# Transposing attention weights by products with a diagonal in the opening of a fused attention and two-MLP kernel

## The chip, the cores and the metric

One core of a Trainium2 chip runs the kernel. The metric is the device time of one execution in microseconds (us). Times of several executions are given as their median. A profiled execution has its own time, and beside it the span from its first to its last instruction.

The engines go by short names: PE is TensorE (PEld its weight loads), DVE VectorE, ACT ScalarE, POOL GpSimd, SP SyncE, which here issues nearly all DMAs. Each engine works through its own queue in order.

## The reference

Sliding-window attention with four sink positions, then two MLPs, all float32:

```python
scores = (1 / sqrt(D)) * q @ k.T                 # B, H, S, D = 2, 8, 768, 64
keep = (key < 4) | ((0 <= query - key) & (query - key < 128))
scores = where(keep, scores, -1e9)
a = exp(scores - max(scores))
a = a / (sum(a) + 1e-9)
x = (a @ v)                                      # heads joined: 1536 x 512
h = x @ w_in;  x = (max(h, 0) + alpha * min(h, 0)) @ w_out    # first MLP, d_ff = 2048
h = x @ w_in2; out = (h - tanh(h)) @ w_out2                   # second MLP
```

The weights reach the device as float64 bits, two 32-bit words each, and are turned into float32 there.

## The kernel before

The 1536 tokens are twelve blocks of 128 (NU); a block has eight heads, taken two at a time. Such a pair is a step n, 48 in all (NPAIR). The MLP work goes in chunks of 512 tokens (c) and tiles of 128 hidden units (f). Float32 precision in the big products comes from splitting each operand into a high and a low part.

A step of attention passes through these functions:

- `s_mm(n)` (L274; L268 for the first block): scores of pair n on PE into two PSUM tiles `ps_o`. Keys and queries come in groups G of two pairs, split by `kq_hi` (ACT, L238) and `kq_lo` (DVE, L241).
- `s_max(n, a)` (DVE, L283): mask and running maximum of one head, result in `pq`; then `s_exp(n, a)` (ACT, L292): exponential and row sum.
- `norm_sum(n)`: 1e-9 is added to the two sums on POOL (L298), reciprocal on DVE (L300). `norm(n)` (DVE, L307) multiplies both heads' rows by the reciprocal. `sink_copy(n)` (DVE, L313) gathers the sink columns of two pairs.
- `t_mm(n)` (PE, L324): the normalised rows are transposed, four 128x128 transposes against an identity matrix (two in a sequence's first block), into `ps_t` or `ps_h`; `sink_mm` (L346) transposes the sink columns. `t_ev(n)` (ACT, L331) copies the transposed tile to `pt`, `sink_ev` (ACT, L350) the sinks to `pts`.
- `pv(n)` (PE, L363, L364): value products; in every second pair of the later blocks also the sink products (L367). `x_h` (ACT, L374) and `x_l` (DVE, L379) split the finished block into the first MLP's input.

The opening is a loop over n from 0 to 18 (S_LEAD = 19) with attention alone. The program order is written out by hand, and each engine's queue follows it. In step n PE gets `s_mm(n+1)`, then `keep_busy` (L513, products of zeros whose result nobody reads, eight, one, three and then two of them), `t_mm(n-1)` and `pv(n-2)`. Three tiles of the first MLP's weights are converted in between (CONV0, from steps 6, 10 and 14): two passes on ACT (L73, L75) and two on DVE (L77, L79). From the end of the loop on, a second loop mixes MLP products (L396, L448) with the remaining attention steps; its first MLP product is the 128x512 product of L396 that waits for `x_h` of block 3.

The lines that set the order on PE in the opening:

```python
            if not last:
                s_mm(n + 1)
                tps[n - 1] = ps_tile("th" if n < S_LEAD - 3 else "ht"[n % 2])
                keep_busy({0: 8, 1: 1, 2: 3}.get(n, 2), tps[n - 1])
...
                if not last:
                    t_mm(n - 1)
...
            if 2 <= n < S_LEAD - 2:
                pv(n - 2)
```

Of the kernel before, what the change touches and what calls it, by code (L numbers as in the profile page):

```python
# [9 lines left out]
F32 = mybir.dt.float32  # L10
# [11 lines left out]

S_LEAD = 19
CONV0 = ((0, 6), (1, 10), (2, 14))
B, H, S, D = 2, 8, 768, 64
# [8 lines left out]
SINK = 32  # L34
# [32 lines left out]

def convert_scaled(nc, pair, dst, seen):

    lw, hw = pair[:, :, 0], pair[:, :, 1]  # L70
    top = pair.bitcast(U16)[:, :, 1]
    di = dst.bitcast(I32)
    nc.scalar.activation(out=dst, in_=hw.bitcast(F32), func=AF.Abs, scale=W_UP, accum_out=seen)  # L73
    yield
    nc.scalar.activation(out=lw, in_=top, func=AF.Copy, scale=1.0 / 8192, bias=FLOOR)  # L75
    yield
    nc.vector.scalar_tensor_tensor(di, di, 3, lw, op0=ALU.logical_shift_left, op1=ALU.bitwise_or)  # L77
    yield
    nc.vector.scalar_tensor_tensor(di, hw, SIGN, di, op0=ALU.bitwise_and, op1=ALU.bitwise_or)  # L79
# [58 lines left out]
def fast_path(tc, qk, v, vsink, limits, w1i, w1o, alpha, w2i, w2o, out, outer):  # L138
# [3 lines left out]
    with ExitStack() as ctx:  # L142
# [60 lines left out]
        def conv_w(m, f):  # L203
            raw = stage[m][f % 2]
            if m == 1 and f < 3:
                wf[m, f] = ap.tile([128, 1024], F32, name="wf", tag="wx" if f == 2 else "pq", bufs=1 if f == 2 else 2)
            else:
                wf[m, f] = wp.tile([128, 1024], F32, name="wf", tag="wf", bufs=NF)
            at = m * NF + f
            yield from convert_scaled(nc, raw.rearrange("p (n t) -> p n t", t=2), wf[m, f], seen[:, at:at + 1])  # L210

# [15 lines left out]
        x_t, y_t = {}, {}  # L227
        pq, sums, ptb, pts, vps, sks, sps, tps = {}, {}, {}, {}, {}, {}, {}, {}
        initial = [True]
# [84 lines left out]

        def t_mm(n):
# [35 lines left out]

        def pv(n):
            u, p, b, i, w = geom(n)
# [5 lines left out]
            for a in range(2):  # L359
# [4 lines left out]
                nc.tensor.matmul(d, lhsT=vt[u][:, h * D:(h + 1) * D], rhs=pt[:, a, 1, :], start=p == 0 and i == 0, stop=p == 3 and i < 2)  # L364
            if p % 2 == 1 and i >= 2:
                for pp in (p - 1, p):
                    nc.tensor.matmul(o[:, pp, :], lhsT=vs[:, pp, :], rhs=pts[G], start=False, stop=pp == 3)  # L367

# [210 lines left out]

        def norms(n):  # L580
            norm_sum(n, 0)
            norm_sum(n, 1)
            norm(n)
            sink_copy(n)

        s_mm(0)
        for n in range(S_LEAD):
            last = n == S_LEAD - 1
            a_loads(n)
            if n == 0:  # L590
                kq_hi(0)
            if n in (3, 5):
                s_max(n, 0)
                s_max(n, 1)
                kq_lo(n // 2 + 1)
                if n == 3:
                    k_sinks(0)
# [4 lines left out]
            if n >= 2:  # L602
                t_ev(n - 2)
                if 5 <= n < S_LEAD - 2:
                    splits_hi(n)
            if n not in (3, 5):
                s_max(n, 0)
                s_max(n, 1)
            if n == 1:
                kq_lo(0)  # L610
            if n == 4:
                kq_lo(1)
                k_sinks(1)
            if n >= 6 and not last:
                splits_lo(n - 1)
# [4 lines left out]
            if n in (1, 2):  # L620
                kq_hi(n)
            if n == 4:
                kq_hi(3)
            if n == S_LEAD - 2:
                pv(n - 2)
            if n >= 1:
                norms(n - 1)
                if not last:
                    t_mm(n - 1)
                    if has_sinks(n - 1):  # L630
                        sink_mm(n - 1, n + 1)
            if 2 <= n < S_LEAD - 2:
                pv(n - 2)
            for f, at in CONV0:
                if n == at:
                    conv_start(0, f, 1)
                if n == at + 1:
                    conv_step(0, f)
            if n >= 5 and n % 4 == 1:
                x_h(n - 2)  # L640
            if last:
# [7 lines left out]
            for f, at in CONV0:  # L649
                if at + 1 < n < at + 4:  # L650
                    conv_step(0, f)
# [434 lines left out]
```

## Time and profile before

| | us |
|---|---|
| median of 3 runs | 648.95 (648.41 to 650.08) |
| the profiled execution | 648.51 |
| its span | 646.7 |
| PE busy | 632.7 (98% of the span) |
| DVE busy | 520.6 (81%) |
| ACT busy | 469.6 (73%) |
| POOL busy | 24.2 (4%) |

A span lies some 2 us below the time of its execution. Busy time of PE counts each matmul up to a modelled end, so that overlapping tails can make it look full; the starts of its instructions say more than its busy share. In a timeline a row is a run of like instructions of one engine: start, length from the first start to the last end, engine, line, operation, tiles, and in brackets the idle time before it with what ended that.

### The profile page before, as it was taken

The page shows a single profiled execution, that of the slowest core. Times are in us where ns is not written, and L with a number is a line of the kernel's source. Part 1 is how long each engine was busy: PE and PEld are TensorE (multiplying, and loading weights), DVE is VectorE, ACT ScalarE, POOL GpSimd, SP SyncE. Part 2 cuts the span into 40 slices and gives each one's busy share as a digit, 9 for nine tenths or more (in the row PEclk, how much of TensorE's full clock was granted, in tenths as well). Part 3 has the DMA queues.
Part 4 walks back from the last instruction along what each step waited for, and adds up shares of the span by engine and source line. Part 5 has one row for each costly group of instructions (what it writes and reads, how often), then busy time and mean ns, then how long its engine had stood idle before and what let it go on. Part 6 is the DMA issues. An engine that isn't in the chain of part 4 may idle for free.

```text
span 646.7 us, 9269 instructions
## 1 busy us (share of the span) xinstructions
PE 632.7 (98%) x3245; PEld 499.5 (77%) x3245; DVE 520.6 (81%) x1046; ACT 469.6 (73%) x936; POOL 24.2 (4%) x57
## 2 busy tenths in 40 slices
PE   8899999999999999999999999999999999999996
PEld 3556777777777777777888888888888888888884
DVE  7998989997676665578999969888898888888883
ACT  6998888886675555568877768777777777777772
POOL 1001101110000000000000000000000000000000
PEclk9999999999999999999999999999999999999998
DMA  5753444651100000323555300000010000100001
GB/s 151 237 184 116 147 166 172 216 162 35 49 3 16 17 1 1 131 71 125 205 195 192 125 1 1 1 1 1 1 66 1 2 2 0 66 0 2 0 2 70
DMA packets 27176, 47.36 MB, mean 73 GB/s; under 512 B 3184, under 2 KB 15728, under 8 KB 27120
## 3 DMA queue, kind: packets, MB, share of 16 engines
q1 hardware_dynamic: 26400, 46.29, 21.1%
q8 instruction: 27, 0.44, 0.3%
q10 hardware_dynamic: 720, 0.39, 0.2%
q14 instruction: 29, 0.24, 0.1%
HBM read 43.53 MB, written 3.15 MB: 72 GB/s over the span
## 4 chain that ended last, share of the span: by engine, by line
PE 89%; ACT 3%; DVE 3%; SPq 2%; issue 1%; DMA 1%; POOL 0%; ACTq 0%; DVEq 0%
PE ps_o L448 39%; PE ps_h L396 23%; PE ps_s L396 9%; PE ps_t L396 8%; PE ps_s L274 2%; PE ps_t L324 2%; PE ps_v L363 2%; SPq L177 1%; PE ps_v L364 1%; PE ps_v L367 1%; ACT pq L292 1%; DVE pq L283 1%; DMA raw<-in_moe_w_out_dram 1%; DVE wf L77 1%; DVE pq L307 0%
## 5 line engine op out<-in xcount | busy, mean ns | idle before, releaser
L224 DVE SCALAR_TENSOR_TENSOR wl<-wf,wh 128x512 fp32r<-128x512 f32 x192 | 123.5, 683 | 42.8 <-ACT wh L219 42.8
L219 ACT ACTIVATE wh<-wf 128x512 fp32r<-128x512 f32 x192 | 110.8, 628 | 0.1
L396 PE MATMUL ps_h<-x,wh 128*128 128x512 f32 x296 | 96.4, 406 | 0.4 <-ACT x L374 0.3
L448 PE MATMUL ps_o<-gh,wh 128*128 128x512 f32 x192 | 76.5, 398 | 0.0
L448 PE MATMUL ps_o<-gh,wl 128*128 128x512 f32 x192 | 75.0, 391 | 0.0
L448 PE MATMUL ps_o<-gl,wh 128*128 128x512 f32 x192 | 74.8, 390 | 0.0
L448 PE MATMUL ps_o<-wh,gh 128*128 128x512 f32 x192 | 74.7, 389 | 0.0
L448 PE MATMUL ps_o<-wl,gh 128*128 128x512 f32 x192 | 74.7, 389 | 0.0
L448 PE MATMUL ps_o<-wh,gl 128*128 128x512 f32 x192 | 74.7, 389 | 0.0
L396 PEld LDWEIGHTS ps_h<-x,wh 128*128 128x128 f32 x296 | 52.1, 188 | 11.4 <-issue 1.9
L292 ACT ACTIVATE pq<-pq,nm 128x288 f32<-128x288 f32 (+1 forms) x96 | 48.5, 509 | 14.5 <-DVE nm L283 14.4
L396 PE MATMUL ps_h<-x,wl 128*128 128x512 f32 x148 | 58.4, 394 | 0.4 <-DVE wl L224 0.4
L331 ACT ACTIVATE pt<-ps_t 128x512 f32<-128x512 f32 (+1 forms) x39 | 22.0, 563 | 42.6 <-PE ps_t L324 42.6
L427 ACT ACTIVATE gh<-g 128x512 fp32r<-128x512 f32 x48 | 30.4, 633 | 29.6 <-DVE g L126 29.6
L77 DVE SCALAR_TENSOR_TENSOR wf<-wf,raw 128x1024 int32<-128x1024 int32 x32 | 39.1, 1222 | 7.1 <-ACT raw L75 7.1
L448 PEld LDWEIGHTS ps_o<-gh,wh 128*128 128x128 f32 x192 | 36.1, 188 | 8.4 <-issue 1.4
L448 PEld LDWEIGHTS ps_o<-gh,wl 128*128 128x128 f32 x192 | 36.0, 188 | 7.8
L448 PEld LDWEIGHTS ps_o<-wh,gh 128*128 128x128 f32 x192 | 36.0, 188 | 7.5
L448 PEld LDWEIGHTS ps_o<-wh,gl 128*128 128x128 f32 x192 | 36.0, 188 | 7.5
L448 PEld LDWEIGHTS ps_o<-wl,gh 128*128 128x128 f32 x192 | 36.0, 188 | 7.5
L448 PEld LDWEIGHTS ps_o<-gl,wh 128*128 128x128 f32 x192 | 36.1, 188 | 7.1
L126 DVE COPY_PREDICATED g<-mask,t 128x512 f32<-128x512 int32 x48 | 36.4, 759 | 4.9
(156 smaller groups left out, 1354.0 us busy)
## 6 DMA issues: line engine op xcount, KB each, us to landing
raw<-in_moe_w_in_dram SPq DMA_DIRECT2D x32, 512.0 KB, 3.3
raw<-in_moe_w_out_dram SPq DMA_DIRECT2D x32, 512.0 KB, 4.2
raw_qk<-in_qk_dram SPq DMA_DIRECT2D x92, 64.0 KB, 3.1
vt<-in_v_dram SPq DMA_DIRECT2D x12, 256.0 KB, 3.1
out_dram<-ob SPq DMA_DIRECT2D x2, 1024.0 KB, 4.2
out_dram<-ob SPq DMA_DIRECT2D x3, 256.0 KB, 2.1
vs<-in_vsink_dram SPq DMA_DIRECT2D x2, 256.0 KB, 4.3
raw_qk<-in_qk_dram ACTq DMA_DIRECT2D x4, 64.0 KB, 2.7
```

The lines of the kernel that those rows point to most:

```text
L77: nc.vector.scalar_tensor_tensor(di, di, 3, lw, op0=ALU.logical_shift_left, op1=ALU.bitwise_or)
L126: nc.vector.copy_predicated(g, mask.bitcast(I32), t)
L219: nc.scalar.activation(out=hi, in_=src, func=AF.Copy, scale=W_DOWN)
L224: nc.vector.scalar_tensor_tensor(lo, wf[m, f][:, 512 * part:512 * part + 512], W_DOWN, hi, op0=ALU.mult, op1=ALU.subtract)
L274: nc.tensor.matmul(sps[n, a][:, :w], lhsT=kq[l][h, p, at:at + 128], rhs=kq[r][h, p, K_EVEN:K_EVEN + w], start=e == 0, stop=e == 2)
L292: nc.scalar.activation(out=e, in_=e, func=AF.Exp, scale=-1.0, bias=nm[:, 2 * n + a:2 * n + a + 1], accum_out=sums[G][:, hh:hh + 1])
L324: nc.tensor.transpose(t[:, 256 * a + 128 * e:256 * a + 128 * e + 128], pq[G][:, hh + a, c:c + 128], ident)
L331: nc.scalar.activation(out=ptb[n][:, :, e0:, :], in_=tv[:, :, e0:, :], func=AF.Copy)
L363: nc.tensor.matmul(d, lhsT=vt[u - 1][:, h * D:(h + 1) * D], rhs=pt[:, a, 0, :], start=p == 0, stop=False)
L396: nc.tensor.matmul(h_ps[f], lhsT=w, rhs=x[:, r, kk, :], start=at == 0, stop=at == 11)
L427: nc.scalar.activation(out=gh, in_=mid[f], func=AF.Copy)
L448: nc.tensor.matmul(o, lhsT=l, rhs=r, start=f == 0 and e == 0, stop=f == NF - 1 and e == 2)
```

## The change

- For the pairs n < DIAG = 18 the rows of `pq` are no longer normalised. `norm` makes two diagonal matrices on POOL instead, the identity times the reciprocal of the row sums, and `t_mm` multiplies `pq` with them as float32 products: transposition and scaling in one. `sink_copy` multiplies the sink columns by the reciprocal on DVE.
- For the first three weight tiles the conversion's second pass moves from ACT to DVE, as one pass of tensor_scalar followed by the two-input pass.
- `keep_busy` gets eight, two, four, two and then none.
- The order in the opening is written anew: from step 5 `pv(n-2)` stands ahead of `s_mm(n+1)`, the sink products are a part of their own (`pv_sinks`) behind it, the sums and diagonals of pair n-1 stand between the two maxima of step n, `x_h` stands ahead of the transposes, and the key splits are called from two small tables.

```diff
+DIAG = 18
...
-def convert_scaled(nc, pair, dst, seen):
+def convert_scaled(nc, pair, dst, seen, by_vector=False):
...
+    if by_vector:
+        nc.vector.tensor_scalar(di, di, 4, 1, op0=ALU.logical_shift_left, op1=ALU.logical_shift_right)
+        yield
+        nc.vector.scalar_tensor_tensor(di, lw, 29, di, op0=ALU.logical_shift_right, op1=ALU.bitwise_or)
...
         def norm(n):
             u, p, b, i, w = geom(n)
             G, hh = 2 * u + p // 2, 2 * (p % 2)
+            if n < DIAG:
+                dg[n] = gp.tile([128, 2, 128], F32, name="dg", tag="gg", bufs=6)
+                for a in range(2):
+                    nc.gpsimd.tensor_scalar(dg[n][:, a, :], ident, sums[G][:, hh + a:hh + a + 1], None, op0=ALU.mult)
+                return
...
-                nc.vector.tensor_copy(sks[G], pq[G][:, :, 128:160])
+                if n < DIAG:
+                    nc.vector.tensor_tensor(sks[G], pq[G][:, :, 128:160], sums[G].unsqueeze(2).to_broadcast([128, 4, SINK]), op=ALU.mult)
...
-                    if i > 0 or e == 1:
-                        nc.tensor.transpose(t[:, 256 * a + 128 * e:256 * a + 128 * e + 128], pq[G][:, hh + a, c:c + 128], ident)
+                    d = t[:, 256 * a + 128 * e:256 * a + 128 * e + 128]
+                    if n < DIAG and (i > 0 or e == 1):
+                        nc.tensor.matmul(d, lhsT=pq[G][:, hh + a, c:c + 128], rhs=dg[n][:, a, :], start=True, stop=True)
...
+            if 2 <= n:
+                t_ev(n - 2)
+                if 5 <= n < S_LEAD - 2:
+                    keys_hi(n)
...
+            if n >= 5 and n < S_LEAD - 2:
+                pv(n - 2, False)
...
-                keep_busy({0: 8, 1: 1, 2: 3}.get(n, 2), tps[n - 1])
+                keep_busy({0: 8, 1: 2, 2: 4, 3: 2}.get(n, 0), tps[n - 1])
...
                 s_max(n, 0)
+                if n > 3:
+                    norm_parts(n - 1)
                 s_max(n, 1)
...
+            elif n >= 5 and not last:
+                pv_sinks(n - 2)
+            if n >= 5 and n % 4 == 1:
+                x_h(n - 2)
...
-            if 2 <= n < S_LEAD - 2:
+            if 2 <= n < 5:
                 pv(n - 2)
```

On PE, before, from the scores of step 10 on: scores, idle products, the transposes of pair 9 with its sinks (`sk`), the value products of pair 8 (`pt`, `vt`), the scores of step 11.

```order
L274 MATMUL ps_o<-kq 128x288 x6
L513 LDWEIGHTS idle
L513 MATMUL ps_t<-idle 128x512
L513 LDWEIGHTS idle
L513 MATMUL ps_t<-idle 128x512
L324 MATMUL ps_t<-ident,pq 128x128 x4
L346 MATMUL ps_o<-ident,sk 128x128
L363 MATMUL ps_v<-pt,vt 64x128
L364 MATMUL ps_v<-pt,vt 64x128
L363 MATMUL ps_v<-pt,vt 64x128
L364 MATMUL ps_v<-pt,vt 64x128
L274 MATMUL ps_o<-kq 128x288 x6
```

The value products there are those of the pair before the one just transposed. The same place on PE in the changed kernel, from the scores of step 10 on (`dg` is the diagonal):

```order
L280 MATMUL ps_o<-kq 128x288 x6
L339 MATMUL ps_t<-dg,pq 128x128 x4
L363 MATMUL ps_o<-ident,sk 128x128
L380 MATMUL ps_v<-pt,vt 64x128
L381 MATMUL ps_v<-pt,vt 64x128
L380 MATMUL ps_v<-pt,vt 64x128
L381 MATMUL ps_v<-pt,vt 64x128
L280 MATMUL ps_o<-kq 128x288 x6
L389 MATMUL ps_v<-pts,vs 128x128 x2
L339 MATMUL ps_h<-dg,pq 128x128 x4
```

Now the value products behind the transposes are those of pair 9 itself, the sink products of pair 9 (L389) follow the next scores, and the idle products are gone.

On DVE, before, in step 8: key split, reciprocal and normalisation of pair 7, first DVE pass of a conversion, the two maxima of step 9.

```order
L241 TENSOR_TENSOR kq<-raw_qk,kq 128x2x256
L300 RECIPROCAL sums<-sums 128x2
L307 TENSOR_SCALAR pq<-pq,sums 128x288 x2
L77 SCALAR_TENSOR_TENSOR wf<-wf,raw_90 128x1024
L283 ISA pq,nm<-ps_o,m_even 128x288
L283 ISA nm 128x1
L283 ISA pq,nm<-ps_o,m_even 128x288
```

The same place on DVE in the changed kernel:

```order
L247 TENSOR_TENSOR kq<-raw_qk,kq 128x2x256
L79 SCALAR_TENSOR_TENSOR wf<-raw_90,wf 128x1024
L289 ISA pq,nm<-ps_o,m_even 128x288
L289 ISA nm 128x1
L306 RECIPROCAL sums<-sums 128x2
L289 ISA pq,nm<-ps_o,m_even 128x288
```

The normalisation is gone, the reciprocal stands between the two maxima of the next step, and the conversion's pass here (L79) is the second of three on DVE.

## Rows read from the trace of the kernel before

**Rows 1.** Page, span in 40 slices, busy tenths; PEclk: granted clock, tenths.

```profile
PE   8899999999999999999999999999999999999996
...
DVE  7998989997676665578999969888898888888883
...
PEclk9999999999999999999999999999999999999998
```

**Rows 2.** Windows, four steps: stretch, its length, then busy us (instructions), as headed.

```profile
core 0: us, PE busy (x) PEld busy (x) DVE busy (x) ACT busy (x) POOL busy (x), PEclk, DMA share, GB/s
25.82:36.67 10.85, 9.84 (x86) 6.18 (x86) 10.54 (x36) 10.40 (x30) 1.20 (x5) 1.00 0.71 218
```

**Rows 3.** Timeline of PE, one step: start, length, line, operation, tiles, shapes, count.

```profile
35.74 0.60 PE L324 MATMUL ps_t<-ident,pq 128*128 128x128 f32 x4
...
36.38 0.45 PE L363 MATMUL ps_v<-pt,vt 128*64 128x128 f32 x4
...
36.98 0.67 PE L274 MATMUL ps_o<-kq 64*128 64x288 f32 x6
37.58 0.60 PE L513 MATMUL ps_h<-idle 128*128 128x512 bf16 x2
38.05 0.72 PE L324 MATMUL ps_h<-ident,pq 128*128 128x128 f32 x4
```

**Rows 4.** Timeline of PE, other places; the x3 row is cut by a narrow window.

```profile
16.40 0.53 PE L274 MATMUL ps_o<-kq 64*128 64x288 f32 x4 [1.02 <-DVE kq L241]
...
18.20 0.66 PE L274 MATMUL ps_o<-kq 64*128 64x288 f32 x6
...
45.53 0.71 PE L367 MATMUL ps_v<-pts,vs 128*128 128x128 f32 x4 [0.53 <-ACT pts L350]
...
45.75 0.50 PE L367 MATMUL ps_v<-pts,vs 128*128 128x128 f32 x3
...
46.18 0.66 PE L274 MATMUL ps_o<-kq 64*128 64x288 f32 x6
47.54 0.59 PE L513 MATMUL ps_h<-idle 128*128 128x512 bf16 x2 [0.70 <-ACT pt L331]
...
52.32 0.50 PE L396 MATMUL ps_h<-x,wh 128*128 128x512 f32 x1 [0.25 <-ACT x L374]
```

**Rows 5.** Single lines, 17 to 47 us: duration ns min/median/max, first and last start.

```profile
L324 PE MATMUL ps_h<-ident,pq x24: 272/273/334, 17.3 to 44.1; 128*128 128x128 f32 x24
...
L367 PE MATMUL ps_v<-pts,vs x12: 275/275/377, 34.1 to 46.0; 128*128 128x128 f32 x12
...
L331 ACT ACTIVATE pt<-ps_h x6: 577/591/612, 18.8 to 46.9; 128x512 f32<-128x512 f32 x6
```

**Rows 6.** Groups by line and shape, 0 to 52 us: busy us, mean ns | idle before.

```profile
L292 ACT ACTIVATE pq<-pq,nm 128x288 f32<-128x288 f32 x28 | 14.8, 535 | 0.3 <-DVE nm L283 0.3
...
L307 DVE TENSOR_SCALAR pq<-pq,sums 128x288 f32<-128x288 f32 x26 | 8.5, 367 | 0.5
...
L73 ACT ACTIVATE wf<-raw 128x1024 f32<-128x1024 f32 x3 | 3.4, 1145 | 0.0
```

**Rows 7.** Timeline of ACT: key copy of step 5; evacuation ahead of TensorE's 47.54.

```profile
15.48 0.63 ACT L238 ACTIVATE kq<-raw_qk 128x512 fp32r<-128x512 f32 x1 [0.32 <-DMA raw_qk<-in_qk_dram]
...
46.90 0.59 ACT L331 ACTIVATE pt<-ps_h 128x512 f32<-128x512 f32 x1
```

**Rows 8.** Timelines of POOL, and of DVE around POOL's addition at 38.86.

```profile
2.00 0.29 POOL masks.py:199 TENSOR_SCALAR_AFFINE_SELECT ident<-ident 128x128 f32<-128x128 f32 x1
...
38.86 0.62 POOL L298 TENSOR_SCALAR sums<-sums 128x2 f32<-128x2 f32 x1 [1.99 <-ACT pq L292]
...
46.08 0.21 POOL L298 TENSOR_SCALAR sums<-sums 128x2 f32<-128x2 f32 x1 [3.63 <-ACT pq L292]
...
38.19 1.22 DVE L79 SCALAR_TENSOR_TENSOR wf<-raw,wf 128x1024 int32<-128x1024 int32 x1
```

**Rows 9.** Windows, columns as in rows 2: early in the opening, and after the end.

```profile
10.00:20.00 10.00, 8.07 (x65) 4.84 (x66) 9.31 (x40) 7.06 (x23) 1.19 (x4) 1.00 0.74 235
...
642.00:644.00 2.00, 0.00 (x0) 0.00 (x0) 0.00 (x0) 0.00 (x0) 0.00 (x0) 0.83 0.44 143
```

More of the change, by code (lines that the diff above doesn't have):

```diff
@@ L74, in convert_scaled @@
     yield
-    nc.scalar.activation(out=lw, in_=top, func=AF.Copy, scale=1.0 / 8192, bias=FLOOR)
-    yield
-    nc.vector.scalar_tensor_tensor(di, di, 3, lw, op0=ALU.logical_shift_left, op1=ALU.bitwise_or)
+    if by_vector:
+        nc.vector.tensor_scalar(di, di, 4, 1, op0=ALU.logical_shift_left, op1=ALU.logical_shift_right)
+        yield
+        nc.vector.scalar_tensor_tensor(di, lw, 29, di, op0=ALU.logical_shift_right, op1=ALU.bitwise_or)
+    else:
+        nc.scalar.activation(out=lw, in_=top, func=AF.Copy, scale=1.0 / 8192, bias=FLOOR)
+        yield
+        nc.vector.scalar_tensor_tensor(di, di, 3, lw, op0=ALU.logical_shift_left, op1=ALU.bitwise_or)
     yield
@@ L209, in conv_w @@
             at = m * NF + f
-            yield from convert_scaled(nc, raw.rearrange("p (n t) -> p n t", t=2), wf[m, f], seen[:, at:at + 1])
+            yield from convert_scaled(nc, raw.rearrange("p (n t) -> p n t", t=2), wf[m, f], seen[:, at:at + 1], m == 0 and f < len(CONV0))
         whl = {}
@@ L227, in fast_path @@
         x_t, y_t = {}, {}
-        pq, sums, ptb, pts, vps, sks, sps, tps = {}, {}, {}, {}, {}, {}, {}, {}
+        pq, sums, ptb, pts, vps, sks, sps, tps, dg = {}, {}, {}, {}, {}, {}, {}, {}, {}
         initial = [True]
@@ L322, in t_mm @@
                 for e, c in ((0, 160 - cur), (1, cur)):
-                    if i > 0 or e == 1:
-                        nc.tensor.transpose(t[:, 256 * a + 128 * e:256 * a + 128 * e + 128], pq[G][:, hh + a, c:c + 128], ident)
+                    d = t[:, 256 * a + 128 * e:256 * a + 128 * e + 128]
+                    if n < DIAG and (i > 0 or e == 1):
+                        nc.tensor.matmul(d, lhsT=pq[G][:, hh + a, c:c + 128], rhs=dg[n][:, a, :], start=True, stop=True)
+                    elif i > 0 or e == 1:
+                        nc.tensor.transpose(d, pq[G][:, hh + a, c:c + 128], ident)
         def t_ev(n):
@@ L350, in sink_ev, with pv @@
             nc.scalar.activation(out=pts[n // 2], in_=tps.pop((n, 0))[:, 384:512], func=AF.Copy)
-        def pv(n):
+        def pv(n, sinks=True):
             u, p, b, i, w = geom(n)
@@ L364, in pv, with pv_sinks @@
                 nc.tensor.matmul(d, lhsT=vt[u][:, h * D:(h + 1) * D], rhs=pt[:, a, 1, :], start=p == 0 and i == 0, stop=p == 3 and i < 2)
-            if p % 2 == 1 and i >= 2:
+            if sinks:
+                pv_sinks(n)
+        def pv_sinks(n):
+            u, p, b, i, w = geom(n)
+            if has_sinks(n):
                 for pp in (p - 1, p):
-                    nc.tensor.matmul(o[:, pp, :], lhsT=vs[:, pp, :], rhs=pts[G], start=False, stop=pp == 3)
+                    nc.tensor.matmul(vps[u][:, pp, :], lhsT=vs[:, pp, :], rhs=pts[n // 2], start=False, stop=pp == 3)
         def x_h(n):
@@ L583, in norms, with keys_lo, keys_hi @@
             norm(n)
+        def norms(n):
+            norm_parts(n)
             sink_copy(n)
+        def keys_lo(n):
+            for G in {1: (0,), 2: (1,), 3: (2,), 5: (3,)}.get(n, (n // 2 + 1,) if n > 5 and n % 2 == 0 else ()):
+                kq_lo(G)
+                if G < 2:
+                    k_sinks(G)
+        def keys_hi(n):
+            for G in {0: (0,), 1: (1,), 2: (2,), 4: (3,)}.get(n, (n // 2 + 2,) if n > 4 and n % 2 else ()):
+                kq_hi(G)
         s_mm(0)
@@ L600, in fast_path @@
                 tps[n - 1] = ps_tile("th" if n < S_LEAD - 3 else "ht"[n % 2])
-                keep_busy({0: 8, 1: 1, 2: 3}.get(n, 2), tps[n - 1])
[L602 to L605, printed above, removed]
+                keep_busy({0: 8, 1: 2, 2: 4, 3: 2}.get(n, 0), tps[n - 1])
             if n not in (3, 5):
                 s_max(n, 0)
+                if n > 3:
+                    norm_parts(n - 1)
                 s_max(n, 1)
[L609 to L615, printed above, removed]
+                if n == 1:
+                    keys_lo(n)
             s_exp(n, 0)
@@ L619, in fast_path @@
             s_exp(n, 1)
[L620 to L623, printed above, removed]
+            if n in (1, 4):
+                keys_hi(n)
             if n == S_LEAD - 2:
                 pv(n - 2)
+            elif n >= 5 and not last:
+                pv_sinks(n - 2)
+            if n >= 5 and n % 4 == 1:
+                x_h(n - 2)
             if n >= 1:
-                norms(n - 1)
+                if n <= 3:
+                    norm_parts(n - 1)
+                sink_copy(n - 1)
+                if n == 2 or 6 <= n and not last:
+                    keys_lo(n)
                 if not last:
```

18 lines of the change are left out of this document (8 added, 10 removed).

## The prediction

> **What bounds the kernel now.** I read the page's slices first, then the windows by stretch, then the timelines of TensorE (PE), VectorE (DVE) and ScalarE (ACT) up to the first product of the first MLP. In the slices the reader sees PE at nine tenths almost throughout, and DVE up there with it in the second and third slice of 16 us, in the opening [rows 1]. After the opening PE has next to no holes, so a shift of its first MLP product, which starts at 52.32 us [rows 4], goes to the end of the kernel almost whole. The question is when that product starts.
>
> Inside the opening the pace is one pair of heads ("a step", n) at a time. Two scores products mark it: s_mm(7) starts at 18.20 and s_mm(17) at 46.18, ten steps in 27.98 us, 2.8 us each [rows 4]. The windows show who sets it: in the four steps from 25.82 to 36.67 DVE is busy 10.54 of 10.85 us, ACT 10.40, PE 9.84 (matmul tails counted) [rows 2]. DVE is full, ACT nearly. PE has filler inside: two idle products a step, 0.47 us from their start to the next transpose [rows 3].
>
> The order on PE in that stretch matters most. Transposes of pair n-1 (L324, L346) are followed by the value products of pair n-2 (L363, L364), then by the scores of n+2 (L274) and idle products (L513) [rows 3]. So ACT has a whole step to evacuate the transposes of pair n-1 before PE asks for them.
>
> **The change, part by part.**
>
> *DVE.* Two normalising multiplications a pair go away: 0.367 us each [rows 6], 0.57 us for the two on DVE's queue, so 2.3 us in four steps. The sink copy becomes a two-input multiplication: under 0.1 us more. A conversion gets one more DVE pass (tensor_scalar, 128x1024). No such row exists; it lies between the 128x288 multiplication (0.367) and the two-input pass of 1.22 us on 1024 elements [rows 6, 8]. Either way DVE falls from 10.5 to between 8.7 and 9.6 us in four steps, 2.2 to 2.4 a step. DVE stops being the bound.
>
> *ACT.* Each conversion loses its second pass, which I price like its first, 1.145 us [rows 6], in four steps; ACT falls from 10.40 to about 9.3, or 2.3 a step.
>
> *PE.* A transpose is one matmul record, a float32 product of the same shape two: the code of L367 issues two products a call and the trace has four records [rows 4, 5]. Spacing is the same 0.11 us: (0.60-0.273)/3 for four transposes [rows 3, 5], (0.50-0.275)/2 inside the L367 group [rows 4, 5]. So four transposes (4 x 0.11 = 0.44 to what follows) become eight records (0.87): +0.43 a step. Two idle products less from step 4 on: -0.47. PE's own sum stays: per step 0.60 value products, 0.60 scores, 0.87 transposes, and per two steps 0.65 sink products and about 0.2 for the sinks' transpose, 2.5 on average.
>
> *The order on PE.* This is the term that decides. From step 5 the value products of a pair move ahead of the scores and stand directly behind the transposes of the same pair, as the order of the changed kernel shows. In between lies ACT's evacuation. PE therefore waits in each step, with the scores, sink products and next transposes queued behind the wait, and the following evacuation waits for those transposes: a ring. Its length: from the first transposing record to the last, 7 x 0.11 = 0.76 if none starts late, 0.88 if the second is 0.22 after the first, as in the L367 group [rows 4]; I take 0.82. The last record itself 0.275 [rows 5]. Hand-over to ACT 0.05, evacuation 0.59 [rows 5], hand-over back 0.05 (the evacuation from 46.90 ends at 47.49, PE goes on at 47.54) [rows 4, 7]. Together 1.79. Then value products 0.60 and scores 0.60 [rows 3], and the next transposes begin: 2.99 us. In odd steps the sink products come in as well, 0.65 from start to the next [rows 4], with 0.05 for ACT's sink evacuation behind one exponential: 3.69. DVE (2.4) and ACT (2.3) fit inside both.
>
> From s_mm(7) to s_mm(17) lie five of each: 5 x 2.99 + 5 x 3.69 = 33.4 us, where it is 27.98 now: **+5.4**.
>
> *The start.* ACT's copy of key group 4 waits for its DMA until 15.48 now and would still [rows 7]. Behind it now stand two exponentials, then (moved ahead) a copy of the attention output, of the key copy's shape, then the evacuation. The key copy takes 0.54 to the next instruction [rows 7], an exponential 0.52 (0.535 long [rows 6]): 15.48 + 0.54 + 2 x 0.52 + 0.54 + 0.59 = 18.2, value products 0.60 with the hand-over, so s_mm(7) at 18.9 where it is 18.20: **+0.7**.
>
> *A crowded step.* In step 14 a conversion pass (1.145 [rows 6]) and a weight split (the key copy's shape, 0.5) stand on ACT between the exponentials and the evacuation: 1.04 + 1.65 = 2.7 against 2.35 when the transposes are done: **+0.35**. With a conversion alone (steps 6 and 10) it is 2.2 and hidden.
>
> *The end of the opening.* In steps 16 and 17 the scores s_mm(18) fill the ring's wait. From s_mm(17): scores, transposes and sinks' transpose 1.67, s_mm(18) to 2.27, evacuation done 2.34, value products to 2.99, sink products behind ACT's sink evacuation 3.08 to 3.9, ACT's copy (0.6, the key copy's shape) to 4.5: first MLP product at 4.55. Now it is 52.32 - 46.18 = 6.14 [rows 4]: **-1.6**.
>
> *Behind it.* Pair 17 is transposed among the MLP products, eight records for four: **+0.43**. The DMA issues keep their order on both queues that have them.
>
> *GpSimd.* Two 128x128 multiplications a pair are new. The nearest rows are its affine select of that shape, 0.29, and its 128x2 addition, 0.21 [rows 8]; the ceiling is an addition that began inside a DVE pass of two SBUF inputs and took 0.62, ending with it [rows 8]. With the worst start, just behind the beginning of a 1.22 us pass, the pair takes up to 1.9. The reciprocal of pair n is done some 1.65 us (odd: 2.35) after its step's start, and the transposes that want the diagonal begin a step and 1.2 us after that start, 4.2 us (odd: 4.9): hidden at both ends of the price, and I put it at nothing (the next pair's addition, behind the diagonals on GpSimd's queue, comes a step later). If the ring were not there, a wait of this kind would show. The Trainium skill (SBUF — State Buffer, SBUF: two separate sides) calls the port pair that the two engines share an exclusive lock: the loser blocks for the whole instruction. By that rule the diagonal also holds up DVE's two-input passes; the trace agrees in the one direction it can show, and the sum stays, since DVE has 0.6 us a step to spare.
>
> **Sum:** 5.4 + 0.7 + 0.35 - 1.6 + 0.43 = +5.3 us. The profiled execution took 648.51 us (span 646.7), 0.4 below the median of 648.95; 648.5 + 5.3 = **653.8 us**, slower by 0.8%. The ring's small prices (late first record, hand-overs) are uncertain by 0.16 us a step over about 12 steps, so 651.5 to 656 by itself.
>
> **The rivals.**
>
> *No ring (faster).* Matmul ends are modelled in the trace. If the real transposes end well before the modelled tail and ACT is quicker, PE reaches the value products with the evacuation nearly done. It decides from the point where the wait, 0.9 us by my sum, is under 0.3 us. Then PE's own 2.5 us a step rules: 25.1 for 27.98, so -2.9 + 0.7 - 1.6 + 0.43 = -3.4: **645.1**. For it: all three engines' sums are below 2.8. Against it: the evacuation's 0.59 us is ACT's own record and has no model in it. 0.10.
>
> *Cheap products (no difference).* If a product with a fresh diagonal streams like one transposing record, steps are 2.55 and 3.25, ten of them 29.0 (+1.0), start +0.5, crowded step +0.75, end -2.0, pair 17 nothing: **648.7**. Against it the four records of L367. 0.12.
>
> *Dear products.* If a product costs four transposes, the four take 1.76 and the ring grows by 0.89 in some 12 steps: **664.5**. Rows say two [rows 5]. The Trainium skill (TensorE: Matmul & The Clock Gate, Terms) gives transposing mode as four times faster for FP32, which is this rival. By that rule it would be the forecast; the trace disagrees, with 0.11 us a record for both and twice the records. 0.03.
>
> *The clock falls.* Granted clock is full, 2.4 GHz, in every slice but the last [rows 1], and falls towards 1.2 only in a window in which PE has no instruction at all [rows 9]. It held from 10 to 20 us with PE busy 8.07 of 10 [rows 9] and a wait of 1.02 us [rows 4]. The ring's waits are under 0.9, but there is one in every step and the filler is gone. At half speed PE's 2.5 a step doubles; over a third of the stretch that is +8: **662**. 0.05.
>
> **How the numbers follow.** The ring has 0.70, no ring 0.10, cheap products 0.12, dear products 0.03, the clock 0.05. Faster by over 0.3% (about what a measurement of this kernel can tell from no change): 0.10. Within it: 0.12. Slower: 0.78. The range reaches down to the cheap products and up past the ring's own 656, leaving out 0.18: 648.3 to 657.5.
>
> **What would show it.** Right: between s_mm(7) and s_mm(17) some 33 us; in every step PE idle before the value products, released by ACT's evacuation, 0.6 to 0.9 us; DVE and ACT down to about 7 tenths there; the first MLP product at about 57; the diagonal's two instructions never the last releaser of the transposes from step 6 on. Each step: 128 product records for the 18 pairs with spacing 0.11; ACT's key copy still at 15.5. Wrong: value products that start at once behind the transposes, or transposes waiting for GpSimd, or a clock under 1.0 before 50 us.

## The result, and the profile of the changed kernel

The changed kernel takes 653.52 us (median of 4 runs, 652.84 to 653.74), the kernel before 648.76 us on the same chip (4 runs, 648.41 to 650.08). The ratio is 1.0068, with a 95% interval from 1.005 to 1.0085: slower, by about 4.8 us. The profiled execution took 652.84 us with a span of 651.1 us, 4.4 us more than the span before.

The page, span in 40 slices as in [rows 1]:

```profile
span 651.1 us, 9397 instructions
...
PE   8779999999999999999999999999999999999996
...
DVE  6767998998576665558999969888898888888884
ACT  6777987886575565477877767777777777777772
POOL 5654100110000000000000000000000000000000
PEclk9999999999999999999999999999999999999999
```

The second and third slice show the loss: PE has gone from eight and nine tenths to seven, VectorE from nine in both to seven and six. GpSimd works at half load where it had almost nothing to do. The granted clock stays at its upper level, 2.4 GHz. After the opening the slices of PE read like those before.

The stretch of ten steps that the prediction used, s_mm(7) to s_mm(17), as a window (columns as in [rows 2]):

```profile
19.24:51.58 32.34, 25.15 (x237) 19.73 (x235) 22.84 (x69) 24.20 (x68) 20.39 (x30) 1.00 0.55 180
```

Ten steps take 32.34 us; before they took 27.98. No engine is full: PE is busy 25.15 us, ScalarE 24.20, VectorE 22.84, GpSimd 20.39. The relief of VectorE and ScalarE is there and buys nothing, since everybody waits.

The timeline of PE shows for whom (start, length, line, operation, tiles, shapes, count, idle time and releaser); L280 are the scores, L339 the products that transpose, L380 and L381 the value products, L389 the sink products, L418 the first MLP:

```profile
19.24 0.66 PE L280 MATMUL ps_o<-kq 64*128 64x288 f32 x6
...
25.41 0.67 PE L280 MATMUL ps_o<-kq 64*128 64x288 f32 x6
26.01 1.16 PE L339 MATMUL ps_t<-dg,pq 128*128 128x128 f32 x8
27.91 0.45 PE L380 MATMUL ps_v<-pt,vt 128*64 128x128 f32 x4 [0.75 <-ACT pt L348]
28.18 0.39 PE L381 MATMUL ps_v<-pt,vt 128*64 128x128 f32 x4
28.51 0.66 PE L280 MATMUL ps_o<-kq 64*128 64x288 f32 x6
...
35.29 0.71 PE L389 MATMUL ps_v<-pts,vs 128*128 128x128 f32 x4
35.84 1.06 PE L339 MATMUL ps_h<-dg,pq 128*128 128x128 f32 x8
...
51.58 0.67 PE L280 MATMUL ps_o<-kq 64*128 64x288 f32 x6
...
56.16 0.50 PE L418 MATMUL ps_h<-x,wh 128*128 128x512 f32 x1
```

The eight records of a pair run from 26.01 to 27.17, then PE is idle for 0.75 us until ScalarE has evacuated them, and only then do the value products and the next scores follow. One step is 28.51 - 25.41 = 3.10 us. ScalarE for its part waits for PE:

```profile
15.32 0.62 ACT L244 ACTIVATE kq<-raw_qk 128x512 fp32r<-128x512 f32 x1
...
18.00 0.60 ACT L348 ACTIVATE pt<-ps_h 128x512 f32<-128x512 f32 x1 [0.53 <-PE ps_h L339]
...
27.26 0.60 ACT L348 ACTIVATE pt<-ps_t 128x512 f32<-128x512 f32 x1 [1.47 <-PE ps_t L339]
```

ScalarE sat idle for 1.47 us before the evacuation at 27.26, until the same eight records released it. The waits of the whole stretch, summed (engine, line, releaser: us in total, times, longest):

```profile
PE ps_v L380 <- ACT pt L348: 7.2, 10, 0.7
...
ACT pt L348 <- PE ps_h L339: 4.2, 5, 1.2
ACT pt L348 <- PE ps_t L339: 3.6, 4, 1.5
...
PEld ps_h L339 <- POOL dg L314: 0.2, 1, 0.2
```

PE waits for ScalarE in each of the ten steps, ScalarE for PE in nine, and a weight load waits for GpSimd's diagonal once, 0.2 us. That is not because the diagonal is cheap. GpSimd's timeline:

```profile
36.42 2.63 POOL L314 TENSOR_SCALAR dg<-ident,sums 128x128 f32<-128x128 f32 x2 [0.36 <-DVE sums L306]
...
39.73 1.19 POOL L314 TENSOR_SCALAR dg<-ident,sums 128x128 f32<-128x128 f32 x2 [0.36 <-DVE sums L306]
```

### The profile page after: what moved, and what is told of

It is laid out like the page before. It is cut to its first block, busy times and chain, and to the rows that moved or that the text cites. A ratio compares the mean times of both kernels' runs of the same rounds, so it can differ in the third digit from the quotient of the medians.

```text
span 651.1 us, 9397 instructions
## 1 busy us (share of the span) xinstructions
PE 634.0 (97%) x3282; PEld 506.3 (78%) x3283; DVE 514.1 (79%) x1013; ACT 467.1 (72%) x933; POOL 53.9 (8%) x93
## 3 DMA queue, kind: packets, MB, share of 16 engines
HBM read 43.53 MB, written 3.15 MB: 72 GB/s over the span
## 4 chain that ended last, share of the span: by engine, by line
PE 93%; ACT 3%; issue 1%; POOL 1%; DVE 1%; DMA 1%; SPq 0%; ACTq 0%; DVEq 0%; POOLq 0%
PE ps_o L470 39%; PE ps_h L418 23%; PE ps_s L418 9%; PE ps_t L418 8%; PE ps_v L380 2%; PE ps_s L280 2%; PE ps_t L341 2%; PE ps_v L381 2%; PE ps_v L389 2%; PE ps_o L280 1%; PE ps_h L339 1%; ACT pt L348 1%; PE ps_t L339 1%; DMA raw<-in_moe_w_out_dram 1%; POOL dg L314 1%
## 5 line engine op out<-in xcount | busy, mean ns | idle before, releaser
L418 PE MATMUL ps_h<-x,wh 128*128 128x512 f32 x296 | 96.4, 406 | 0.1
L418 PEld LDWEIGHTS ps_h<-x,wh 128*128 128x128 f32 x296 | 52.1, 189 | 10.9 <-issue 1.9
L418 PE MATMUL ps_h<-x,wl 128*128 128x512 f32 x148 | 58.4, 394 | 0.4 <-DVE wl L230 0.4
L83 DVE SCALAR_TENSOR_TENSOR wf<-wf,raw 128x1024 int32<-128x1024 int32 x29 | 35.4, 1222 | 6.9 <-ACT raw L81 6.9
```

What stands on the lines that cost most here:

```text
L418: nc.tensor.matmul(h_ps[f], lhsT=w, rhs=x[:, r, kk, :], start=at == 0, stop=at == 11)
```

## The experiments

Each kernel was timed beside the kernel before on the same chip. The table gives, from the profile of each, where s_mm(7) and s_mm(17) start, the time between them, the start of the first MLP product, and the timed ratio to the kernel before with its 95% interval.

| kernel | s_mm(7) | s_mm(17) | between | first MLP | ratio |
|---|---|---|---|---|---|
| before | 18.20 | 46.18 | 27.98 | 52.32 | 1 |
| after | 19.24 | 51.58 | 32.34 | 56.16 | 1.0068 [1.005, 1.0085] |
| e1 after, value products later | 19.09 | 51.72 | 32.63 | 60.02 | 1.0085 [1.0068, 1.0101] |
| e2 after, transposes | 20.64 | 59.56 | 38.92 | 64.84 | 1.0144 [1.0088, 1.0199] |
| e3 after, evacuation in halves | 20.18 | 53.10 | 32.92 | 57.68 | 1.0071 [1.0055, 1.0088] |
| e4 before, value products first | 19.71 | 51.12 | 31.41 | 55.92 | 1.0044 [1.0027, 1.0061] |
| e5 as e1, diagonal on VectorE | 18.48 | 47.91 | 29.43 | 55.95 | 1.0044 [1.003, 1.0057] |
| e6 after, diagonal on VectorE | 19.88 | 52.25 | 32.37 | 56.82 | 1.0083 [1.0066, 1.01] |
| e7 before, one head by product | 18.35 | 49.11 | 30.76 | 55.37 | 1.004 [1.0027, 1.0053] |
| e8 after, transposes and idle products | 19.89 | 51.19 | 31.30 | 56.14 | 1.0042 [1.003, 1.0053] |
| e9 before, second pass on VectorE | 18.59 | 46.96 | 28.37 | 52.91 | 1.0009 [0.9999, 1.0019] |
| e10 before, idle products gone | 19.76 | 47.82 | 28.06 | 53.47 | 0.9985 [0.9975, 0.9996] |
| e11 as e1, transposes and idle products | 17.88 | 47.17 | 29.29 | 54.30 | 1.0035 [1.0023, 1.0047] |
| e12 before, idle products till step 8 | 18.32 | 46.31 | 27.99 | 51.96 | 0.9992 [0.9981, 1.0003] |

**The order alone: e4.** Only the value products of the kernel before move, to directly behind the transposes of their own pair (the sink products follow behind the next scores, as in the changed kernel):

```
             a_loads(n)
+            if 5 <= n < S_LEAD - 2:
+                t_ev(n - 2)
+                splits_hi(n)
+                pv(n - 2, False)
...
-            if 2 <= n < S_LEAD - 2:
+            if 2 <= n < 5:
                 pv(n - 2)
```

> The kernel before with one thing of the change: from step 5 the value products of pair n-2 stand ahead of the scores of pair n+1, directly behind their own transposes, the sink products behind the scores. Transposes, normalisation on DVE, conversions and idle products as before. Ring theory: first to last of four transposes 0.33-0.45, tail 0.27, copy and hand-overs 0.70, value products 0.60, scores 0.60, idle products 0.47: about 3.05 us a step and 3.5 with sink products, the stretch 31 to 33 us instead of 28, the time 651.5 to 653. Rival, the products with the diagonal cost the time: 648.8, no change.

652.13 us against 649.31: the ring appears without a diagonal and without a product in place of a transpose, within the times that were expected. The waits of the ten steps:

```profile
PE ps_v L363 <- ACT pt L331: 7.4, 10, 0.8
```

The same ten waits of 0.75 us as in the changed kernel, and 31.41 us for ten steps. The order costs +3.4 us in the stretch by itself.

**The same from the other side: e8 and e2.** The changed kernel with transposes for its products (VectorE normalises again), without idle products (e2) and with those of before (e8):

```
-DIAG = 18
+DIAG = 0
...
-                keep_busy({0: 8, 1: 2, 2: 4, 3: 2}.get(n, 0), tps[n - 1])
+                keep_busy({0: 8, 1: 1, 2: 3}.get(n, 2), tps[n - 1])
```

(The second hunk is in e8 alone.)

> The changed kernel without the diagonal: DVE normalises, PE transposes (four records), in the new order and without the idle products. Ring theory: the ring is there, shorter by 4 records, 0.44 us: 2.65 us in steps without sink products and 3.1 with them, unless DVE, which has the normalisation and the third conversion pass now (2.75 us a step), sets the pace; the stretch takes 28 to 30 us, the time is 649.5 to 651.5. Rival, the products alone cost the time: back at 648.5. Rival, the order alone with no part for the products' length: 653.

> The run with transposes and DVE normalisation in the new order (e2), in which the granted clock was half from 10 to 44 us, with the idle products of the kernel before put back (8, 1, 3, then 2 a step). If the missing idle products let the clock fall there, it is full in this run; then only the ring is left, 0.33 + 0.27 + 0.70 + 1.20 + 0.45 = 3.0 us a step and 3.45 with sink products: stretch 31 to 32 us, time 651.5 to 653.5. If the clock falls again: 657 or more.

e8 takes 652.17 us against 649.2, and 31.30 us for ten steps, again with ten waits for the evacuation:

```profile
PE ps_v L380 <- ACT pt L348: 7.3, 10, 0.8
```

Both lie in the ranges that were expected. Its plain step is 2.98 us, its step with sink products 3.43. So products in place of transposes and idle products add 0.11 us to a step of the ring. e2 missed its range of 649.5 to 651.5: it takes 658.64 us, with a 95% interval of the ratio from 1.0088 to 1.0199. Its windows:

```profile
10.00:44.00 34.00, 27.82 (x166) 18.42 (x165) 25.56 (x96) 21.72 (x65) 2.83 (x10) 0.61 0.57 182
```

And the same stretch in e8:

```profile
10.00:44.00 34.00, 26.02 (x219) 16.89 (x222) 30.63 (x112) 25.84 (x77) 4.23 (x12) 1.00 0.62 190
```

The granted clock is 0.61 of full in e2, most of the stretch at 1.2 GHz, and 1.00 in e8. So in this order the clock held with transposes and idle products and with the float32 products of the changed kernel, and fell with transposes and no idle products.

**The order undone alone: e1.** The changed kernel with the value products back behind the next pair's transposes:

```
-            if n >= 5 and n < S_LEAD - 2:
-                pv(n - 2, False)
...
-            if 2 <= n < 5:
+            if 2 <= n < S_LEAD - 2:
                 pv(n - 2)
```

> The changed kernel with one thing put back: the value products of pair n-2 stand behind the transposes of pair n-1 again, on PE, with their sink products and the copy of the attention output. Products with the diagonal, three DVE passes a conversion and the missing idle products stay. Ring theory: the wait of PE for ACT's evacuation (0.75 us a step) is gone; the pace is then set by an engine's own sum (PE 2.4, ACT 2.3, DVE 2.3, POOL about 2.3 us a step), s_mm(7) to s_mm(17) takes 25 to 28 us instead of 32.3, and the time falls by 4 to 6 us, to 647.5 to 650. Rival, the products themselves cost the time (PE's work on transposes doubles): the order matters little, the stretch stays above 31 us and the time at 652 or more.

The expectation was missed: 655.06 us against 649.31, no gain at all. PE's waits for the evacuation are gone, and others stand in their place:

```profile
DVE sums L306 <- POOL sums L304: 9.2, 10, 1.9
...
PE ps_h L339 <- POOL dg L314: 2.7, 7, 0.7
PE ps_t L339 <- POOL dg L314: 2.5, 4, 1.1
```

GpSimd and PE at one place:

```profile
25.15 2.43 POOL L314 TENSOR_SCALAR dg<-ident,sums 128x128 f32<-128x128 f32 x2 [0.36 <-DVE sums L306]
27.67 0.22 POOL L304 TENSOR_SCALAR sums<-sums 128x2 f32<-128x2 f32 x1
28.26 1.92 POOL L314 TENSOR_SCALAR dg<-ident,sums 128x128 f32<-128x128 f32 x2 [0.37 <-DVE sums L306]
```

```profile
27.64 0.71 PE L339 MATMUL ps_t<-dg,pq 128*128 128x128 f32 x4 [1.11 <-POOL dg L314]
```

VectorE has the key split (25.27) and a conversion pass (25.98) one behind the other in this place, and a pair of diagonals takes 2.43 us. PE has transposed the first head and waits 1.11 us for the second diagonal. The next pair's addition (27.67) had to wait behind the diagonals on GpSimd's queue, then came the reciprocal, then the next diagonals. That happens in two of the ten steps; in the other eight the addition waits for ScalarE's exponentials, 8.7 us in all. Ten steps take 32.63 us, as long as with the ring. The profiled run also lost time behind s_mm(17), where PE waited 1.32 us for a diagonal: between 53 and 58 us the granted clock averages 0.68.

**The diagonal taken off GpSimd: e5 and e6.** One word changes, in e1 (e5) and in the changed kernel (e6):

```
-                    nc.gpsimd.tensor_scalar(dg[n][:, a, :], ident, sums...
+                    nc.vector.tensor_scalar(dg[n][:, a, :], ident, sums...
```

> The run with the value products put back behind the transposes of the next pair (e1), and the diagonals made on DVE (0.26 to 0.29 us each) instead of POOL (0.61 each, more when a DVE pass with two SBUF inputs holds it up). Theory of two rings one behind the other: without PE's ring the time is held by a second one, exponential, POOL's addition, reciprocal, POOL's diagonals (1.4 to 2.6 us), transposes, evacuation, next exponentials; with DVE's diagonals it is over 1 us shorter in two steps, and DVE's own sum of 2.7 to 2.8 us a step sets the pace: stretch 27 to 29 us, time 648.5 to 650.5. Rival, the doubled transposing work of PE is what holds e1 at 655: no change, 654 to 656.

> The changed kernel with the diagonals made on DVE instead of POOL, and nothing else. Ring theory: in the order of the changed kernel PE's wait for the evacuation hides POOL, so that a faster diagonal gives nothing: stretch 32 to 32.8 us, time 653 to 654. Rival, POOL's diagonals cost the time already there: down by 1 us or more for each 0.1 us a step, to 651 or less.

e6, 654.94 us (653 to 654 were expected), is no faster than the changed kernel: 32.37 us for ten steps instead of 32.34, and PE waits 7.2 us for the evacuation as before. In the ring, what GpSimd takes is hidden. e5 takes 652.31 us, 2.75 less than e1, and 29.43 us for ten steps. The wait for the addition on GpSimd, 9.2 us in e1, falls with it:

```profile
DVE sums L306 <- POOL sums L304: 2.9, 4, 1.1
```

So GpSimd's chain held up e1, for 3.2 of its 32.63 us. But e5 misses its 648.5 to 650.5: something more than those two is slower than before. Part of it is the clock. In the profiled run it averages 0.76 from 50 to 57 us, behind a wait of PE of 1.65 us that ended at 53.37, so the first MLP product of that run is not compared. Of the eight runs, the four with a mean clock of 0.998 took 651.12 to 651.94 us, the four with 0.994 or 0.995 took 652.68 to 653.16.

**Half a dose of GpSimd: e7.** The kernel before in its own order, where only the second head of a pair goes by a diagonal and a product, with one idle product less:

```
+            if n < DIAG:
+                dg[n] = gp.tile([128, 128], F32, name="dg", tag="gg", bufs=6)
+                nc.gpsimd.tensor_scalar(dg[n], ident, sums[G][:, hh + 1:hh + 2], None, op0=ALU.mult)
-            for a in range(2):
+            for a in range(1 if n < DIAG else 2):
...
+                    if a == 1 and n < DIAG and (i > 0 or e == 1):
+                        nc.tensor.matmul(..., rhs=dg[n], start=True, stop=True)
```

> The kernel before, with its order, in which one head of each pair (n < 18) is transposed by products with a POOL diagonal and the other is normalised on DVE as before; its sink columns are multiplied on DVE in two small instructions; one idle product a step instead of two. A candidate to beat both. DVE loses 0.28 us a step and gets 0.1 back; POOL makes one diagonal (0.61, up to 2.0 behind a DVE pass). If DVE's sum sets the pace of the kernel before: stretch 26 to 27 us, time 646.5 to 648. If a chain through POOL takes over at once, as in e1: 649 to 652.

651.55 us against 649.2: the second of the two cases. The chain through GpSimd shows even with one diagonal a pair:

```profile
POOL dg L308 <- DVE sums L301: 3.7, 6, 0.9
PEld ps_h L334 <- POOL dg L308: 3.5, 5, 1.3
...
DVE sums L301 <- POOL sums L299: 2.6, 5, 0.8
```

**The ring made shorter: e3.** The changed kernel with the evacuation in two copies, one for each head:

```
-            nc.scalar.activation(out=ptb[n][:, :, e0:, :], ...)
+            for a in (slice(0, 1), slice(1, 2)) if 3 <= n < S_LEAD - 4 else (slice(0, 2),):
+                nc.scalar.activation(out=ptb[n][:, a, e0:, :], ...)
```

> The changed kernel, with the evacuation of pairs 3 to 14 on ACT cut into two copies, one for each head (0.36 us each, 0.26 from start to start, instead of 0.60). Ring theory: the value products of the first head start behind the first copy, 0.24 us earlier in each of 10 to 12 steps, so PE's wait falls from 0.75 to about 0.5 and the time by 2.3 to 2.9 us, to about 651. Rivals in which another engine or the products set the pace: no change, or 12 x 0.02 us slower for ACT's extra instructions.

Missed: 654.16 us. PE's timeline:

```profile
25.62 0.43 PE L381 MATMUL ps_v<-pt,vt 128*64 128x128 f32 x2 [0.53 <-ACT pt L349]
25.89 0.27 PE L382 MATMUL ps_v<-pt,vt 128*64 128x128 f32 x1
...
26.16 0.38 PE L382 MATMUL ps_v<-pt,vt 128*64 128x128 f32 x2
26.48 0.66 PE L280 MATMUL ps_o<-kq 64*128 64x288 f32 x6
```

The wait does fall, from 0.75 to 0.53 us. But the value products now take 26.48 - 25.62 = 0.86 us to the scores instead of 0.60 (28.51 - 27.91): the two heads' records ran side by side and now the second head comes later. A step is 3.14 us.

**What is left of the change: e11 and e9.** e11 is e1 with transposes and the idle products of before (both hunks of e8). e9 is the kernel before with the conversions' second pass on VectorE alone:

```
+        nc.vector.tensor_scalar(di, di, 4, 1, op0=ALU.logical_shift_left, op1=ALU.logical_shift_right)
+        yield
+        nc.vector.scalar_tensor_tensor(di, lw, 29, di, op0=ALU.logical_shift_right, op1=ALU.bitwise_or)
```

> The changed kernel with the value products put back behind the next pair's transposes, the transposes back for the float32 products, and the idle products of before. What is left of the change: the second pass on VectorE, the multiplications between the two maxima, the new order of the key work. Theory (order on TensorE plus products and diagonals are all of the loss): s_mm(7) to s_mm(17) takes 27.5 to 28.7 us, the time is 648 to 649.5. Rival (the moved VectorE and key work costs too): over 29 us there and 650 or more.

> The kernel before with one part of the change alone: the second pass of the three early conversions goes from ScalarE to VectorE (1.14 us less on ScalarE, 0.69 us more on VectorE, in steps 7, 11 and 15). Theory (VectorE sets the pace of the opening before, 10.54 of 10.85 us busy in four steps): each pass costs its 0.69 us, three make +2, so 650.5 to 651. Rival (ScalarE, 10.40 of 10.85, is the bound in exactly those steps): 647 to 648. No difference (648.5 to 649.5) would say that the steps with a conversion have VectorE time to spare.

e9: 649.54 us against 648.98, no difference within 0.3%, so neither theory nor rival; the steps with a conversion have some time to spare on VectorE. e11: 651.36 us, the rival. Without ring, product or diagonal, and with idle products, 1.3 us are lost in the stretch and 1.0 us behind it (54.30 - 47.17 = 7.13, before 6.14). The runs of e5 that kept the clock, 651.12 to 651.94 us, lie beside this median, so as far as these runs tell, diagonals on VectorE and float32 products add next to nothing of their own in this order. VectorE in e11:

```profile
26.46 0.45 DVE L289 CUSTOM_DVE_ANT_0 pq<-ps_o,m_even 128x288 f32<-128x288 f32 x1
...
27.03 0.65 DVE L318 TENSOR_SCALAR pq<-pq,sums 128x288 f32<-128x288 f32 x2
27.60 0.45 DVE L289 CUSTOM_DVE_ANT_0 pq<-ps_o,m_even 128x288 f32<-128x288 f32 x1
```

In the kernel before, the two maxima of a pair:

```profile
25.82 0.45 DVE L283 CUSTOM_DVE_ANT_0 pq<-ps_o,m_even 128x288 f32<-128x288 f32 x1
...
26.20 0.45 DVE L283 CUSTOM_DVE_ANT_0 pq<-ps_o,m_even 128x288 f32<-128x288 f32 x1
```

And ScalarE in e11:

```profile
26.96 0.54 ACT L298 ACTIVATE pq<-pq,nm 128x288 f32<-128x288 f32 x1 [0.49 <-DVE nm L289]
...
28.09 0.54 ACT L298 ACTIVATE pq<-pq,nm 128x288 f32<-128x288 f32 x1 [0.51 <-DVE nm L289]
```

The reciprocal and the multiplications of the pair before now lie between the two maxima of a pair (26.46 and 27.60), which stood back to back, and ScalarE's exponentials wait for both maxima. Over the opening such waits add up to 5.4 us in e11, to nothing in the changed kernel, and to 0.3 us in the kernel before [rows 6] (first line e11, second line the changed kernel):

```profile
L298 ACT ACTIVATE pq<-pq,nm 128x288 f32<-128x288 f32 x28 | 14.8, 531 | 5.4 <-DVE nm L289 5.4
...
L298 ACT ACTIVATE pq<-pq,nm 128x288 f32<-128x288 f32 x28 | 14.6, 526 | 0.0
```

It was not tried alone whether this place makes up the 2.4 us, rather than the new order of the key work or the conversions' second pass on VectorE.

**The idle products: e10 and e12.** The kernel before without its idle products from step 3 on (e10), or from step 8 on (e12):

```
-                keep_busy({0: 8, 1: 1, 2: 3}.get(n, 2), tps[n - 1])
+                keep_busy({0: 8, 1: 1, 2: 3, 3: 2}.get(n, 0), tps[n - 1])
```

(e12: `.get(n, 2 if n < 8 else 0)`.)

> The kernel before with one part of the change alone: the two idle products of a step are gone from step 3 on; transposes stay. If transposes do not carry the clock, the granted clock goes to half somewhere between 15 and 50 us, PE's records there last 1.5 to 2 times as long, and the time is 653 to 658. Rival (in this order PE has enough else to do): the clock stays at 1.00, PE only waits longer for VectorE, and the time is 648.5 to 649.5.

> The kernel before without the two idle products of a step from step 8 on; up to step 7 they stay. In e10, which dropped them from step 3 on, the profiled run lost about 2 us at half clock from 17.4 to 24 us and the runs with the least of that took 646.9 to 647.9. Theory (the idle products cost a little wherever PE is the last to come, and are needed only around the wait for the key group's DMA): the clock stays at 1.00 through the opening and the time is 647 to 648. Rival (VectorE sets the pace after step 8, so the products lie in time in which PE would wait): 648.7 to 649.3, no difference. Second rival: the clock falls later instead, 650 or more.

e10's profiled run did fall to half clock, behind a wait of PE of 1.01 us that ended at 17.43, and came back:

```profile
18.00:24.00 6.00, 6.00 (x35) 4.03 (x34) 4.56 (x17) 4.12 (x10) 0.42 (x2) 0.50 0.81 244
```

That run, 650.04 us, is the slowest of e10's twelve. Their median is still 648.26 us against 648.98, just below the rival's range. The ratio of 0.9985 is a gain of 0.15%, clear of its interval but small; no run shows where it comes from. In e12's profiled run the clock holds at 1.00 through the opening (two of the twelve runs, 649.80 and 650.14 us, have a mean clock of 0.993 and 0.992), and the median is 648.29 against 649.12: between the two ranges, with an interval that includes no difference. The waits of PE tell why there is so little to gain, first in e12:

```profile
PE ps_t L324 <- DVE pq L307: 3.5, 3, 1.4
...
PE ps_h L324 <- DVE pq L307: 2.5, 4, 0.9
```

And in the kernel before:

```profile
PE ps_t L324 <- DVE pq L307: 1.6, 3, 0.8
```

With the 0.2 us of its other tile that is 1.8 us in the kernel before; in e12 PE waits 6.0 us for VectorE's multiplications. In the kernel before the idle products lie in that time, and the stretch is 27.98 or 27.99 us either way. No version of these twelve is faster than the kernel before by more than 0.3%.

## Why the prediction was right, point by point

**What bounds, and where the loss goes.** Right on where the loss goes. It lies before the first MLP product but for 0.56 us: that product starts 3.84 us later (56.16 - 52.32), and from there to the end are 594.94 us instead of 594.38. That PE did not set the pace before is borne out by e12, where PE only waits longer for VectorE. That VectorE alone set it is not shown: three more passes of 0.69 us on it (e9), with ScalarE relieved in return, cost no more than 0.2%.

**The ring.** Right in kind and almost in size. Predicted 33.4 us from s_mm(7) to s_mm(17), measured 32.34. The plain step was 2.99 and is 3.09: the eight records take 1.16, so the first comes late as in [rows 4], the upper of the two bounds that were given. The step with sink products was 3.69 and is 3.55. The larger error is in the count: the working charged sink products to five odd steps, but only three of the ten have them, since the pairs 5 and 7 belong to a block without sinks. With three, the working's own prices give 7 x 2.99 + 3 x 3.69 = 32.0. The step with sink products is shorter than its price because they take 0.55 us to the next transposes (35.29 to 35.84) where 0.65 was charged, and the eight records behind them 1.06 instead of 1.16. PE's wait, foreseen at 0.6 to 0.9 us, is 0.75 (0.64 beside a sink transpose). e4 and e8 show that the order makes it, with or without products.

**The start.** +1.04 us where +0.7 was predicted (19.24 against 18.20). The queue on ScalarE is as described, and the key copy at 15.32 came a little earlier than assumed. The evacuation was not late behind that queue, as the working had it: it began at 18.00, after ScalarE had idled 0.53 us until PE's transposes were done. What came late there was PE.

**The crowded step.** Mis-sized: +0.35 predicted, +0.06 measured. From the value products at 44.29 to those at 47.44 are 3.15 us, against 3.09 in a plain step.

**The end, and behind it.** -1.6 predicted, -1.56 measured (56.16 - 51.58 = 4.58, predicted 4.55). Behind it +0.43 predicted, +0.56 measured. Sum of what was measured: 1.04 + 4.36 - 1.56 + 0.56 = +4.4 us, the difference of the spans (the crowded step lies inside the 4.36); predicted +5.3. The medians differ by 4.76 us: the profiled execution of the changed kernel was the quickest of its four, 0.7 us under their median. That the forecast of 653.8 lies only 0.3 from the median of 653.52 is partly luck. With the right count the working's sum is 1.4 less, +3.9 us or 652.4: two steps too many with sink products made up for a plain step and a start that were priced too low.

**The price of a product.** Right: 128 records for the 64 transposes, 0.275 us each and 0.11 us apart. So the rivals of cheap and dear products fall. The Trainium skill (TensorE: Matmul & The Clock Gate, Terms) gives transposing mode as four times faster for FP32. Here it is twice, two records for one of the same spacing.

**VectorE and ScalarE.** The new pass of 128x1024 takes 0.69 us, inside its bounds. Both engines fell to about 0.7 and 0.75 of the stretch, as foreseen.

**GpSimd.** Hidden, as predicted, but the price was wrong. The nearest row of the working was 0.29; a diagonal takes 0.61 (median 608 ns), up to 2.05, and a pair up to 2.63, above the stated ceiling of 1.9. The sentence that such a wait would show if the ring were not there is what e1 and e7 measured: e1 takes 32.63 us for ten steps, as long as with the ring, and 29.43 when the diagonals leave GpSimd (e5). The working did not see that addition, reciprocal and diagonals make a second chain of about that length.

**The clock.** It held at 1.00 in the changed kernel, so that rival falls for this kernel. It is real close by: e2 fell with transposes in the products' place, e1 and e5 with the products, behind longer waits.

**What the prediction did not name.** The changed order on VectorE and of the key work, with the conversions' second pass on VectorE, costs 2.4 us when nothing else is in the way (e11). In the changed kernel it lies under the ring: e8 has it and e4 does not, and their ten steps take 31.30 and 31.41 us.

## What to carry to other kernels

Before moving a step next to the one that feeds it, add up the loop that arises: transposes, hand-over, evacuation, hand-over, consumers; if that sum is longer than the busiest engine's step, the loop is the new pace, however much each engine was relieved. Several loops can lie under each other at nearly the same length, so undoing one part of a slow change may show no gain (e1, e6) though that part is slow by itself (e4, e7). And filler that lies in time in which its engine would wait for another is nearly free: taking it away changed the time by 0.15% (e10) and by 0.1%, no clear difference (e12).

## What the runs showed of the hardware

**GpSimd beside VectorE.** A 128x128 multiplication of GpSimd takes 0.60 us undisturbed (597 ns at the least) and 2.05 at the most, when VectorE's passes with two SBUF inputs follow each other (36.42 in the changed kernel). VectorE loses little in return: in e1 the low half of the keys (L247) took at most 795 ns and the last conversion pass 1333, where they took at most 694 and 1227 before. The Trainium skill (SBUF — State Buffer, SBUF: two separate sides) has the pair of ports as an exclusive lock that goes to whichever starts first, for the whole instruction. That a diagonal of GpSimd that began inside such a pass stood still through the next one too (2.05 us, from 37.01) agrees. In the other direction the trace differs: in e1 a diagonal ran from 25.15 to 25.76, and the key split on VectorE that began at 25.27 took 0.80 us instead of 0.69, and not the 0.49 us more that waiting for the end of the diagonal would have cost.

**The same multiplication on VectorE** takes 0.28 us (median 284 ns in e5), less than half.

**Value products of two heads** that write different halves of the output's partitions overlap: eight records in 0.60 us, and in e3, with the second head held back, 0.86.

**The granted clock.** In the same order it averaged 0.61 over 34 us with transposes (e2), and stayed at 1.00 with transposes and idle products (e8) or with float32 products and no idle products (the changed kernel), where PE waits 0.75 us a step. With float32 products and no idle products it also fell to 1.2 GHz at the end of the opening of e1 and e5, behind waits of PE of 1.32 and 1.65 us: 0.68 on average from 53 to 58 us in e1, 0.76 from 50 to 57 in e5. In e10, with transposes and no idle products, it fell behind a wait of 1.01 us; in the kernel before, with idle products, it held through one of 1.02 [rows 4].
